# Who shares a wide tile with whom: group sums and gate batches in a fused attention and MLP kernel

## The chip, the cores and the metric

The kernel runs on one core of a Trainium2 chip. The metric is the device time of one execution in microseconds (us); a comparison uses the median of several executions. Times inside the kernel come from one profiled execution, counted from the start of its span. TensorE appears in the profile as PE (matmuls) and PEld (weight loads), VectorE as DVE, ScalarE as ACT, GpSimd as POOL, SyncE's queue as SPq. SyncE issues nearly all transfers.

## The reference

Linear attention without a softmax, an RMS norm over each head, and then a two-layer network whose gate is `h * erf(softplus(h))`:

```python
# q, k, v: (8, 8, 576, 64); w_in: (512, 2048), w_out: (2048, 512); float64 weights for the network
kv  = np.einsum('bhsd,bhse->bhde', k, v)
out = np.einsum('bhsd,bhde->bhse', q, kv)
rms = np.sqrt(np.mean(out * out, axis=-1, keepdims=True) + 1e-06)
x   = (out / rms * g_norm)           # -> (4608, 512): rows are tokens
h   = x @ w_in
sp  = np.maximum(h, 0.0) + np.log1p(np.exp(-np.abs(h)))
g   = h * erf(sp)
y   = g @ w_out                      # (4608, 512)
```

## The kernel before

The 4608 tokens are worked through in nine groups `T` of 512 (`NG = 9`). In each group the 2048 hidden features are 16 blocks of 128, taken in batches of four (`BATCH = 4`, so `NB = 4` batches in a group). The first two groups (`FIRST = 2`) run a plain fp32 path while the weights are converted and cut into three forms; from group 2 on, and for the last batch of group 1, a product of fp32 precision is put together from three cheaper matmuls (`n_ps` takes eight matmuls, `m_ps` four).

From there on the kernel is a loop over batches `m`, with `T, b = divmod(m, 4)`. It starts at `m = 8`. In iteration `m` the hidden products of batch `m` are computed into a wide tile `h`; the gates of batch `m - 1`, made in the iteration before, are cut into forms and multiplied by their four blocks of `w_out`; and the result is added to the group's sums `es`, which are stored to the output after the group's last batch. Since the results trail by one batch, the first group that the loop stores is group 1: its sums were begun before the loop, and are finished and stored in iteration 8.

The wide tiles are of one size: 128 partitions by 4 x 512 fp32 values. There are three of them: two in the pool `wide`, given out in turns under the tag `h`, and one in the pool `acc` under the tag `e`. A tile that is given out again must wait until all that read the former contents is done.

```python
    wide = ctx.enter_context(tc.tile_pool(name="wide", bufs=2, side="right"))
    ...
            acc = ctx.enter_context(tc.tile_pool(name="acc", bufs=1))
    ...
    # the plain path: who takes a wide tile, in order of time
                    xT[T] = wide.tile([P, KC, G], FP32, name="xT", tag="h")          # T = 0, 1
                x_high = wide.tile([P, KC, G], FP32R, name="x_high", tag="h")        # group 1
                old_h = acc.tile([P, BATCH, G], FP32, name="h", tag="e")             # last batch of group 1
                    x_both = wide.tile([P, KC, G], FP32R, name="x_both", tag="h")    # group 1
                sums(*((acc, "e") if T2 < FIRST - 1 else (wide, "h")))               # groups 0 and 1

    def sums(pool, tag):
        all_e = pool.tile([P, J, DM], FP32, name="e", tag=tag)
        ...                               # es[j] = all_e[:, j], copied from o_ps[j]

    def store(T, j, e):
        if T < B:
            rows = out[T * S : T * S + G, :].rearrange("(p j) f -> p j f", j=J)
            nc.sync.dma_start(out=rows[:, j, :], in_=e)
            return
        ...

    def product(weights, moving, turns=True):     # L462 is its matmul
        ...                               # two of six PSUM banks in turns: n_ps (8 matmuls), m_ps (4)

    def result(T, b, j, g, w):
        ps = product(...)
        if b == 0:
            if j == 0:
                all_e = acc.tile([P, J, DM], FP32, name="e", tag="e")
                es.update((i, all_e[:, i]) for i in range(J))
            nc.vector.tensor_scalar(                                                 # L775
                out=es[j], in0=ps[0], scalar1=SHIFT - 1.0, scalar2=None, op0=ALU.mult
            )
        else:
            add_scaled(es[j], ps[0], SHIFT - 1.0)                                    # L440
        add(es[j], ps[1])                                                            # L445

    for m in range(first_batch, batches + 1):
        ...
        g, done = g_next, len(g_next)
        g_next = []
        if m < batches:
            h = wide.tile([P, BATCH, G], FP32, name="h", tag="h")
            s = gate_r.tile([P, BATCH, G], FP32, name="s", tag="s")
        for i in range(BATCH):
            if m < batches:
                n_ps, m_ps = hidden(T, b * BATCH + i)
            fetch(i)                                  # weight parts for later, on SyncE's queue
            if i == 0:
                for half in range(done, 2):
                    g.append(cut_upper(old_h, half))                                 # ACT, L405
            if done <= i < 2:
                cut_lower(old_h, i, g[i])                                            # DVE, L408 and L411
            if m < batches:
                nc.scalar.activation(h[:, i], n_ps, AF.Copy, scale=SHIFT - 1.0)      # L834
                add(h[:, i], m_ps)                                                   # L445
                nc.scalar.activation(s[:, i], h[:, i], AF.Softplus)                  # L836
            pieces(i + 1)                             # a piece of the next group's attention
        ...                                           # Erf of s (L840)
        for j in range(J):
            result(T2, b2, j, g, w)
            fetch(BATCH + j)
            if b2 == NB - 1:
                store(T2, j, es.pop(j))
            ...                                       # h *= s (L854), pieces of attention
        old_h = h
```

Of the kernel before, what the change touches and what calls it, by code (L numbers as in the profile page):

```python
# [39 lines left out]
FP32 = mybir.dt.float32  # L40
FP32R = mybir.dt.float32r
# [9 lines left out]
BATCH = 4  # L51
# [3 lines left out]
FIRST = 2  # L55
# [5 lines left out]
def kernel(  # L61
# [11 lines left out]
    P = 128  # L73
    B, H, S, D = q.shape
    DM, DF = moe_w_in.shape[0], moe_w_in.shape[1] // 2
    J = 4
    G = J * P
    R = S - G
    NP = H // 2
    KC = DM // P  # L80
# [6 lines left out]
    attp = ctx.enter_context(tc.tile_pool(name="attp", bufs=1))  # L87
    dram = ctx.enter_context(tc.tile_pool(name="dram", bufs=1, space=bass.MemoryType.DRAM))

    wide = ctx.enter_context(tc.tile_pool(name="wide", bufs=2, side="right"))  # L90

    room, early_room, low_room = (ctx.enter_context(ExitStack()) for _ in range(3))
    first_w = room.enter_context(tc.tile_pool(name="first_w", bufs=1, side="right"))
# [162 lines left out]
    def weights():  # L256

        w_next("split")
        w_next("join")
        w_next("load")  # L260


    xT, x_forms, tails = {}, {}, {}
# [5 lines left out]
    def attention(T, p, pools=None):  # L269
# [94 lines left out]
        def norm():  # L364
            ms, u, r = (st.pop(name) for name in ("ms", "u", "r"))
            nc.vector.scalar_tensor_tensor(
                out=u, in0=ms, scalar=EPS, in1=u, op0=ALU.add, op1=ALU.mult
            )
            nc.vector.scalar_tensor_tensor(
                out=u, in0=u, scalar=3.0, in1=r, op0=ALU.subtract, op1=ALU.mult  # L370
            )
            if T < FIRST:
                if T not in xT:
                    xT[T] = wide.tile([P, KC, G], FP32, name="xT", tag="h")
                x = xT[T][:, p, :]
            else:
                x = st["x"] = x_new.tile([P, G], FP32, name="x", tag="x")
            nc.vector.scalar_tensor_tensor(
                out=x,
                in0=st.pop("o"),  # L380
                scalar=gm_col,
                in1=u,
                op0=ALU.mult,
                op1=ALU.mult,
            )
# [153 lines left out]
# [4 lines that stand above are left out]
            e = es[j] = all_e[:, j]  # L543
            if j % 2:
                nc.scalar.copy(e, o_ps[j])
            else:
                nc.vector.tensor_copy(out=e, in_=o_ps[j])
# [87 lines left out]
    def due(k):  # L635

        i = w_at["join"] + k
        ahead = 1 if LAG - 2 <= n < LAG + BATCH else 2
        return i < len(w_order) and w_order[i][0] <= n + ahead

    def gates(n):
        nc.vector.tensor_tensor(out=hs[n], in0=hs[n], in1=ss[n], op=ALU.mult)  # L642

    for n in range(FIRST * FC + 1):
        T, f = divmod(n, FC)
        if n == FC:
            early_room.close()
            late = ctx.enter_context(tc.tile_pool(name="late", bufs=1))
            x_new = ctx.enter_context(tc.tile_pool(name="x_new", bufs=1))
            acc = ctx.enter_context(tc.tile_pool(name="acc", bufs=1))  # L650
            w_in_p = ctx.enter_context(tc.tile_pool(name="w_in_p", bufs=BATCH))
            low = low_room.enter_context(tc.tile_pool(name="low", bufs=1))
            forms = late.tile([P, 3, KC, G], FP32R, name="x_forms0")
            x_forms[FIRST] = [forms[:, i] for i in range(3)]
        if T < FIRST:
            if f == 0:
                steps = pieces_of(T + 1)
            if due(1):
                weights()
            for key in list(w_new)[:2]:  # L660
                w_lower(*key)
            for piece in steps[f][0]:
                piece()
        while due(0):
            weights()
        done = n - LAG + 1
        if T == 0 and done >= 0:
            gates(done)
        if T == FIRST - 1:
            if f == 0:  # L670
                x_high = wide.tile([P, KC, G], FP32R, name="x_high", tag="h")
                x_low = low.tile([P, KC, G], FP32R, name="x_low")
                for i in range(0, KC, 2):
                    upper(xT[T][:, i : i + 2], x_high[:, i : i + 2])
                for i in range(0, KC, 2):
                    lower_only(xT[T][:, i : i + 2], x_high[:, i : i + 2], x_low[:, i : i + 2])
        if T == FIRST - 1 and f >= WHOLE:
            n_ps, m_ps = hidden(T, f, turns=False)
        elif T < FIRST:

            if n > 1:
                plain[n] = ps_h.tile([P, G], FP32, name="h_ps", tag="h")
                blocks = [(n, c) for c in range(KC)]
            elif n == 0:
                for i, (pool, tag) in enumerate(((ps_at, "at"), (ps_o, "o0"))):
                    plain[i] = pool.tile([P, G], FP32, name="h_ps", tag=tag)
                blocks = [(i, c) for c in range(KC - 1) for i in range(2)] + [(0, KC - 1)]
            else:
                blocks = [(1, KC - 1)]
            for i, c in blocks:  # L690
                nc.tensor.matmul(  # L691
                    plain[i],
                    lhsT=w_in_sb[:, c, i % FC * P : i % FC * P + P],
                    rhs=xT[T][:, c, :],
                    start=(c == 0),
                    stop=(c == KC - 1),
                )
        if T < FIRST:
            if n == whole:
                old_h = acc.tile([P, BATCH, G], FP32, name="h", tag="e")  # L700
            h = hs[n] = old_h[:, n - whole] if n >= whole else unit("h_sb")
            s = ss[n] = unit("s_sb")
            if n in plain:
                nc.scalar.copy(h, plain.pop(n))
            else:
                nc.scalar.activation(h, n_ps, AF.Copy, scale=SHIFT - 1.0)
                add(h, m_ps)
            if T == FIRST - 1:
                if f == 1:
                    x_both = wide.tile([P, KC, G], FP32R, name="x_both", tag="h")  # L710
                    for i in range(0, KC, 2):
                        both_only(x_high[:, i : i + 2], x_low[:, i : i + 2], x_both[:, i : i + 2])
                    x_forms[T] = x_high, x_low, x_both
                gates(done)
                for key in list(w_new):
                    w_lower(*key)
                for key in to_cut[f]:
                    w_upper(*key)
            nc.scalar.activation(s, h, AF.Softplus)
            if n == 0:  # L720
                w_next("split")
            for piece in steps[f][1]:
                piece()
            if f % BATCH == BATCH - 1:
                for i in range(n - BATCH + 1, n + 1):
                    nc.scalar.activation(ss[i], ss[i], AF.Erf)
                softplus_table()
            if T == FIRST - 1:
                load_parts("in", {FC - 3: 2, FC - 2: 1, FC - 1: 1}.get(f, 0))
        if n >= LAG:  # L730
            T2, f2 = divmod(n - LAG, FC)
            last = n - LAG in (FC - 1, whole - 1)
            project(f2, hs[n - LAG], last)
            if last:
                sums(*((acc, "e") if T2 < FIRST - 1 else (wide, "h")))
                if T2 == 0:
                    for j in range(J):
                        store(T2, j, es.pop(j))
        if T < FIRST:
            for piece in steps[f][2]:  # L740
                piece()
# [23 lines left out]
    def result(T, b, j, g, w):  # L765

        ps = product(
            lambda form, f: g[j // 2][:, form, f, j % 2 * P : j % 2 * P + P],
            lambda form, f: w[f][:, form],
        )  # L770
        if b == 0:
            if j == 0:
                all_e = acc.tile([P, J, DM], FP32, name="e", tag="e")
                es.update((i, all_e[:, i]) for i in range(J))
            nc.vector.tensor_scalar(  # L775
                out=es[j], in0=ps[0], scalar1=SHIFT - 1.0, scalar2=None, op0=ALU.mult
# [4 lines that stand above are left out]
# [5 lines left out]
    for m in range(first_batch, batches + 1):  # L786
        T, b = divmod(m, NB)
        todo = []
        if T + 1 < NG:
            todo = list(attention(T + 1, b))  # L790
            if b == 0:
                side = late_r if T % 2 == FIRST % 2 else late
# [3 lines left out]
        def piece():  # L796
            if todo:
                todo.pop(0)()
# [20 lines left out]
        g, done = g_next, len(g_next)  # L819
        g_next = []  # L820
        if m < batches:
            h = wide.tile([P, BATCH, G], FP32, name="h", tag="h")
            s = gate_r.tile([P, BATCH, G], FP32, name="s", tag="s")
        for i in range(BATCH):
            if m < batches:
# [17 lines left out]
        T2, b2 = divmod(m - 1, NB)  # L843
# [50 lines left out]
```

## Time and profile before

| | before |
|---|---|
| device time, median of 3 | 954.99 us (953.88 to 955.01) |
| span of the profiled execution | 952.2 us, 11746 instructions |
| TensorE matmuls busy | 929.1 us, 98% |
| VectorE busy | 740.4 us, 78% |
| ScalarE busy | 616.1 us, 65% |
| bytes moved by DMA | 259.78 MB, mean 273 GB/s |

How to read it: a busy share near 100% says which engine is in use all along, and not that every microsecond of it is needed. Where a stage of the kernel is paced by TensorE, time can only be won by removing matmul work or idle stretches of TensorE. The chain of waits follows the work that ended last back from the end, at each step to what released it. The list of waits names who stood idle for whom. A table of windows gives the busy time of each engine in chosen stretches of time, with TensorE's granted clock and the share of the 16 DMA engines in use.

### The profile page before, as it was taken

Reading aid. Unit: us, or ns where it says so; the run is one execution under the profiler, and the core shown is the slowest. Engines: PE = TensorE matmul, PEld = TensorE weight load, DVE = VectorE, ACT = ScalarE, POOL = GpSimd, SP = SyncE. Lnnn points to the kernel's source line nnn. Section 1 sums busy time; section 2 is a strip of 40 time slices with the busy share of each in tenths; the row PEclk is TensorE's granted clock in tenths of the full one; section 3 lists DMA queues with packets and bytes.
Section 4 is the critical chain, followed back from the end, with each engine's and each line's share of the span. In section 5 each row is a group of like instructions: output and inputs, shape, how many; then the busy total and the mean of one; then the engine's idle time right before and its main releaser. Section 6 shows DMA issues by size and latency. Waiting matters only on the chain.

```text
span 952.2 us, 11746 instructions
## 1 busy us (share of the span) xinstructions
PE 929.1 (98%) x4272; PEld 684.7 (72%) x4272; DVE 740.4 (78%) x1054; ACT 616.1 (65%) x825; POOL 2.4 (0%) x10
## 2 busy tenths in 40 slices
PE   6999999999998999999999999999999999999998
PEld 4444445665686788888888888888888788878886
DVE  3979958888575888888888888887887877777667
ACT  3889876777665666666666666666666666665552
POOL 1000000000000000000000000000000000000000
PEclk9999999999999999999999999999999999999999
DMA  9856505899699888898899988988896779768872
GB/s 256 276 163 212 167 9 218 307 347 337 212 356 339 275 286 282 289 315 301 290 304 309 303 293 314 322 290 283 290 337 251 264 256 348 283 248 304 338 272 65
DMA packets 111842, 259.78 MB, mean 273 GB/s; under 512 B 43864, under 2 KB 69544, under 8 KB 111784
## 3 DMA queue, kind: packets, MB, share of 16 engines
q1 hardware_dynamic: 110152, 256.73, 78.1%
q10 hardware_dynamic: 1568, 2.29, 0.8%
q8 instruction: 34, 0.56, 0.2%
q14 instruction: 24, 0.20, 0.1%
q0 software_dynamic: 64, 0.00, 0.0%
HBM read 224.40 MB, written 34.60 MB: 272 GB/s over the span
## 4 chain that ended last, share of the span: by engine, by line
PE 83%; ACT 6%; DVE 6%; DMA 3%; SPq 1%; issue 1%; DVEq 0%; ACTq 0%
PE n_ps L462 42%; PE m_ps L462 21%; PE o_ps L520 8%; PE h_ps L691 3%; PE se_ps L325 3%; PE kv_ps L297 2%; PE qt_ps L319 2%; DMA out_dram<-e 1%; DMA w_in_parts<-w_in 1%; SPq L136 1%; ACT w_e L215 1%; ACT L103 1%; DVE h L445 1%; ACT w_m L219 1%; DMA q_sb<-in_q_dram 1%
## 5 line engine op out<-in xcount | busy, mean ns | idle before, releaser
L462 PE MATMUL n_ps<-x_forms,w_in_parts 128*128 128x512 f32 x896 | 234.9, 404 | 5.0 <-ACT h L834 3.4
L462 PE MATMUL n_ps<-w_out_parts,g_forms 128*128 128x512 f32 x928 | 231.3, 391 | 0.0
L462 PEld LDWEIGHTS n_ps<-x_forms,w_in_parts 128*128 128x128 f32 x896 | 167.6, 189 | 49.4 <-issue 9.3
L462 PEld LDWEIGHTS n_ps<-w_out_parts,g_forms 128*128 128x128 f32 x928 | 174.2, 188 | 38.4 <-issue 1.7
L836 ACT ACTIVATE s<-h 128x512 f32<-128x512 f32 x112 | 71.1, 635 | 180.5 <-DVE h L445 180.5
L445 DVE TENSOR_TENSOR h<-m_ps,h 128x512 f32<-128x512 f32 x116 | 79.8, 688 | 68.3 <-ACT h L834 48.9
L462 PE MATMUL m_ps<-w_out_parts,g_forms 128*128 128x512 f32 x464 | 124.2, 389 | 0.0
L462 PE MATMUL m_ps<-x_forms,w_in_parts 128*128 128x512 f32 x448 | 120.0, 390 | 0.0
L520 PE MATMUL o_ps<-w_out_sb,h_sb 128*128 128x512 f32 x224 | 100.8, 593 | 0.3 <-DVE h_sb L642 0.3
L462 PEld LDWEIGHTS m_ps<-w_out_parts,g_forms 128*128 128x128 f32 x464 | 87.1, 188 | 18.1
L462 PEld LDWEIGHTS m_ps<-x_forms,w_in_parts 128*128 128x128 f32 x448 | 84.3, 188 | 17.8
L445 DVE TENSOR_TENSOR e<-m_ps,e 128x512 f32<-128x512 f32 x116 | 80.2, 692 | 17.9 <-PE m_ps L462 10.5
L440 DVE SCALAR_TENSOR_TENSOR e<-n_ps,e 128x512 f32<-128x512 f32 x88 | 60.3, 685 | 37.6 <-PE n_ps L462 37.5
L520 PEld LDWEIGHTS o_ps<-w_out_sb,h_sb 128*128 128x128 f32 x224 | 42.3, 190 | 48.9 <-issue 46.6
L834 ACT ACTIVATE h<-n_ps 128x512 f32<-128x512 f32 x112 | 65.6, 586 | 13.4 <-DMA out_dram<-e 9.5
L411 DVE SCALAR_TENSOR_TENSOR g_forms<-g_forms 128x1024 fp32r<-128x1024 f32 x58 | 71.1, 1225 | 2.0
L408 DVE TENSOR_TENSOR g_forms<-h,g_forms 128x1024 fp32r<-128x1024 f32 x58 | 70.6, 1217 | 1.8 <-ACT g_forms L405 1.4
L405 ACT ACTIVATE g_forms<-h 128x1024 fp32r<-128x1024 f32 x58 | 58.9, 1060 | 12.4 <-PE m_ps L462 9.8
L854 DVE TENSOR_TENSOR h<-h,s 128x1024 f32<-128x1024 f32 x56 | 65.9, 1218 | 0.7 <-ACT s L840 0.7
L691 PE MATMUL h_ps<-xT,w_in_sb 128*128 128x512 f32 x144 | 64.9, 594 | 0.8 <-DVE w_in_sb L240 0.6
L106 ACT ACT_TABLE_LOAD x44 | 56.5, 1283 | 0.7
L840 ACT ACTIVATE s<-s 128x1024 f32<-128x1024 f32 x56 | 56.2, 1052 | 0.3
(98 smaller groups left out, 1014.9 us busy)
## 6 DMA issues: line engine op xcount, KB each, us to landing
w_out_parts<-w_out SPq DMA_DIRECT2D x116, 768.0 KB
w_in_parts<-w_in SPq DMA_DIRECT2D x112, 768.0 KB
w_in<-w_new SPq DMA_DIRECT2D x16, 768.0 KB
q_sb<-in_q_dram SPq DMA_DIRECT2D x32, 256.0 KB
w_raw<-in_moe_w_out_dram SPq DMA_DIRECT2D x8, 1024.0 KB
out_dram<-e SPq DMA_DIRECT2D x32, 256.0 KB
k_sb<-in_k_dram SPq DMA_DIRECT2D x28, 287.5 KB
v_sb<-in_v_dram SPq DMA_DIRECT2D x28, 287.5 KB
```

The costliest lines, as they stand in the source:

```text
L106: nc.scalar.preload_act_table_set("softplus")
L405: nc.scalar.activation(high, x, AF.Copy, scale=1.0 + 2.0**-13)
L408: nc.vector.tensor_tensor(out=low, in0=x, in1=high.bitcast(FP32), op=ALU.subtract)
L411: nc.vector.scalar_tensor_tensor(out=both, in0=low.bitcast(FP32), scalar=SHIFT, in1=high.bitcast(FP32), op0=ALU.mult, op1=ALU.add,)
L440: nc.vector.scalar_tensor_tensor(out=out_, in0=ps, scalar=scale, in1=out_, op0=ALU.mult, op1=ALU.add)
L445: nc.vector.tensor_tensor(out=out_, in0=ps, in1=out_, op=ALU.add)
L462: nc.tensor.matmul(ps, lhsT=weights(form, k), rhs=moving(form, k), start=(form == forms[0] and k == 0), stop=(form == forms[-1] and k == 3),)
L520: nc.tensor.matmul(o_ps[j], lhsT=g[:, j * P : j * P + P], rhs=w_out_sb[:, f, :], start=(f == 0), stop=last,)
L691: nc.tensor.matmul(plain[i], lhsT=w_in_sb[:, c, i % FC * P : i % FC * P + P], rhs=xT[T][:, c, :], start=(c == 0), stop=(c == KC - 1),)
L834: nc.scalar.activation(h[:, i], n_ps, AF.Copy, scale=SHIFT - 1.0)
L836: nc.scalar.activation(s[:, i], h[:, i], AF.Softplus)
L854: nc.vector.tensor_tensor(out=part(h, half), in0=part(h, half), in1=part(s, half), op=ALU.mult)
```

## The change

The two tiles of the pool `wide` get names of their own, `a` and `b`, in place of turns under one tag. In the plain path each user gets the tile that the turns had given it. In the loop the users are dealt out anew. The group sums always take tile `a`. The gate batches `h` take tile `b` when `m` is even and the tile of `acc` when `m` is odd. What this is for: a batch `h` shall not be given a tile out of which sums are still being stored.

```diff
-    wide = ctx.enter_context(tc.tile_pool(name="wide", bufs=2, side="right"))
+    wide = ctx.enter_context(tc.tile_pool(name="wide", bufs=1, side="right"))
@@ the plain path
-                    xT[T] = wide.tile([P, KC, G], FP32, name="xT", tag="h")
+                    xT[T] = wide.tile([P, KC, G], FP32, name="xT", tag="ab"[T])
-                x_high = wide.tile([P, KC, G], FP32R, name="x_high", tag="h")
+                x_high = wide.tile([P, KC, G], FP32R, name="x_high", tag="a")
-                    x_both = wide.tile([P, KC, G], FP32R, name="x_both", tag="h")
+                    x_both = wide.tile([P, KC, G], FP32R, name="x_both", tag="b")
-                sums(*((acc, "e") if T2 < FIRST - 1 else (wide, "h")))
+                sums(*((acc, "e") if T2 < FIRST - 1 else (wide, "a")))
@@ def result
-                all_e = acc.tile([P, J, DM], FP32, name="e", tag="e")
+                all_e = wide.tile([P, J, DM], FP32, name="e", tag="a")
@@ the loop over batches
-            h = wide.tile([P, BATCH, G], FP32, name="h", tag="h")
+
+            pool, tag = (acc, "e") if m % 2 else (wide, "b")
+            h = pool.tile([P, BATCH, G], FP32, name="h", tag=tag)
```

No operation, transfer or order of instructions is changed; what changes is the address of some operands and, with it, who waits for whom.

## The prediction

> **What bounds the kernel now.** I read the page first, then the list of waits, the chain of waits around the one wait that the change aims at, windows cut at the batches of the loop, and the timelines of TensorE and VectorE there. The page says that the whole is paced by TensorE:
>
> ```profile
> span 952.2 us, 11746 instructions
> PE 929.1 (98%) x4272; PEld 684.7 (72%) x4272; DVE 740.4 (78%) x1054; ACT 616.1 (65%) x825; POOL 2.4 (0%) x10
> ```
>
> The list of waits has many entries for DVE and ACT, which cost nothing while PE runs on. Three lines belong together, each of one single occurrence: ACT stood 9.5 us before L834 for a store of sums, and PE then stood 3.4 us for that L834 (its weight load 3.8 us).
>
> ```profile
> ACT h L834 <- DMA out_dram<-e: 9.5, 1, 9.5
> ...
> PEld n_ps L462 <- ACT h L834: 3.8, 1, 3.8
> ...
> PE n_ps L462 <- ACT h L834: 3.4, 1, 3.4
> ```
>
> The chain (start us, us, what) shows the same place as the only piece longer than 3 us after 280 us that is not PE's: the last store, issued at 283.21, lands 9.85 us later, and L834 follows at once.
>
> ```profile
> 283.21 9.85 DMA out_dram<-e
> 293.21 0.61 ACT h L834
> ```
>
> Next, windows cut where PE begins the hidden products of iterations 8, 9, 10, 11 and 12 (256.18, 280.90, 311.80, 336.53, 361.36). The reader is to see that iteration 9 alone takes 30.90 us, and that PE's clock is below 1 in it:
>
> ```profile
> 256.18:280.90 24.72, 24.72 (x129) 19.98 (x128) 18.66 (x28) 16.81 (x23) 0.00 (x0) 1.00 0.85 297
> 280.90:311.80 30.90, 27.00 (x131) 21.18 (x129) 19.11 (x27) 15.83 (x21) 0.00 (x0) 0.94 0.93 344
> 311.80:336.53 24.73, 24.73 (x130) 19.98 (x128) 20.17 (x30) 16.08 (x22) 0.00 (x0) 1.00 0.85 281
> 336.53:361.36 24.83, 24.83 (x131) 20.09 (x129) 20.19 (x29) 15.94 (x22) 0.00 (x0) 1.00 0.86 295
> ```
>
> Slices of 5 us place the loss of clock and the state of the DMA engines (last two columns: share, GB/s):
>
> ```profile
> 285.00:290.00 5.00, 5.00 (x23) 3.83 (x22) 1.46 (x2) 0.00 (x0) 0.00 (x0) 1.00 1.04 422
> 290.00:295.00 5.00, 1.59 (x6) 0.98 (x5) 1.16 (x2) 1.03 (x2) 0.00 (x0) 0.90 0.97 374
> 295.00:300.00 5.00, 5.00 (x18) 3.98 (x18) 3.42 (x6) 2.37 (x6) 0.00 (x0) 0.76 0.61 182
> ```
>
> PE's timeline shows the stop, and the eight matmuls after it in 3.68 us where iteration 8 has 1.98; VectorE's shows the first write into the next group's sums:
>
> ```profile
> 265.57 1.98 PE L462 MATMUL n_ps<-x_forms,w_in_parts 128*128 128x512 f32 x8
> ...
> 293.86 3.68 PE L462 MATMUL n_ps<-x_forms,w_in_parts 128*128 128x512 f32 x8 [3.41 <-ACT h L834]
> ```
>
> ```profile
> 301.68 0.68 DVE L775 TENSOR_SCALAR e<-n_ps 128x512 f32<-128x512 f32 x1
> ```
>
> [...] PE stands 3.41 us, and the clock averages 0.90 and 0.76 in the two slices above. So the stop costs its own length and a slow stretch after it. [...] a 256 KB store that takes 9.85 us: SyncE issued two 768 KB weight parts at 281.31, just ahead of it, and the engines were at 1.04 of their time and 422 GB/s.
>
> **The change, part by part.**
> 1. The plain path: the turns under one tag gave xT of group 0 the first tile, xT of group 1 the second, then x_high the first, x_both the second, the sums of group 1 the first. The names a, b, a, b, a give the same. Cost 0. Iteration 8's batch took the second, now b: 0 again.
> 2. Iteration 9's batch took the first tile in the old order, and that held the sums of group 1, whose four stores were issued at 274.01, 276.12, 280.92 and 283.21. Now it takes the tile of acc, whose last content, the last batch of group 1, was read by the cuts of iteration 8. They ended at 264.2 on DVE. So L834 no longer waits. ACT is free at 283.69 (L405 at 281.67, two in 2.02 us) and n_ps is complete at 282.9, so L834 can start 9.5 us sooner. VectorE's L445 stands behind the first cut on DVE, which ends at 286.5, as in every iteration (in iteration 10 it starts 6.6 us after PE's start; 280.90 + 6.6 = 287.5). PE needs its bank for the fourth hidden product at 290.46, so it does not stop.
> 3. What that is worth on PE: 30.90 us less the length of an iteration with the same work. Iteration 11 is the fitting one, since both have 131 matmul records and end with the transposition of q_last (L305), and it takes 24.83. Saved: 30.90 - 24.83 = 6.07 us. By parts: 3.41 us of standing still; the clock, (1 - 0.90) x 5 + (1 - 0.76) x 5 = 1.7 us (the timeline's pair gives 3.68 - 1.98 = 1.7 too); and 0.45 us in front of the transposes of q at 311.39, which waited for L378 because ACT and DVE ran late. These are 5.56 us. The remaining 0.5 us are small gaps and the modelled ends of matmuls, which I don't place; I take the difference of the iterations.
> 4. Sums of groups 2 to 8 move from the tile of acc to a, batches from two tiles in turns to b and acc. Each keeps the count it had: one tile for sums, two for batches, with the same readers. Cost 0 in the 27 remaining iterations.
> 5. New in iteration 9: the first L775 of group 2 writes into a, the tile being stored. This is the wait of part 2 in a later place, and the first rival below.
>
> After 312 us PE stands for others 1.4 us in all by the list of waits, so nothing downstream absorbs a shift. Everything after iteration 9 moves forward by 6.07: 952.2 - 6.1 = 946.1 us of span, and 954.99 - 6.07 = 948.9 us of device time.
>
> **The rivals.** First, L775 takes over the wait. In iteration 8 the first read of a result stands 14.13 us after PE's start (270.31 - 256.18), so L775 would be ready at 280.90 + 14.1 = 295.0, and the store was down by 293.2: 1.8 us to spare. In front of that store lie only transfers issued before the stop could make any difference, so its landing should hold. If it were late, DVE has 1.6 us of idle time behind the next result (iteration 8, 1.61 before the second L440), and L378 ends at 279.5, 1.0 us before PE's transposes at 280.49 need it. It would thus have to land later than about 297.5 to be felt. For it speaks only that the DMA engines are full there. It would give 949 to 951.
>
> Second, the transfers become the bound. From 275 to 295 they run at 1.02 or more in most slices, and the stop gave them time to catch up; the share falls to 0.61 after 295. Without the stop, the last two weight parts for iteration 9's results (issued from 281.31, ahead of the store and so down by about 293) are needed from 280.90 + 12.1 = 293.0, the third and fourth about 0.9 and 1.4 us into it. Counting the packets of weight parts in order of issue, I find the last of them through near 290.5. For iteration 10, two parts of w_in are issued at 297.61 and 298.55, behind slow issues of k and v that owe nothing to the stop, with two parts of w_out and k, v among them: 4 x 0.79 + 0.58 = 3.7 MB, at 0.42 MB per us some 9 us, so down by about 307.5. They are needed at 305.73 + 6.25 = 312.0 and 314.7. In both places there is room, in the first only 1 to 3 us. If it fails, PE stops again for 1 to 4 us, perhaps with the half clock: 950 to 954.
>
> Third, the new addresses or the new dealing of tiles make a wait in each iteration, say a batch in acc that waits for its reader two iterations back. The reader is then a whole iteration (24.7 us) past. I see nothing for it; 27 waits of 0.5 us would give 962.
>
> **Range and chances.** The sum gives 948.9. The three times before lie within 1.1 us of each other. I give the first two rivals together 15%, each with a loss of 1 to 3 us, and the third 2%. So the range is 947.8 to 950.8. A gain over 2% would need 19 us, three times all that iteration 9 loses: 1%. A loss over 2% is as unlikely: 1%.
>
> **What would show it.** Right: no wait of L834 for out_dram; iteration 9 at 24.8 us; a granted clock of 1.00 throughout from 285 to 300; the wait of PE for L834 gone; the first L775 of group 2 near 295.0; the same 24.7 and 24.8 in iterations 10 and 11. Wrong in the first rival's way: DVE waiting for out_dram in front of L775 and PE standing near 304. In the second's: PE waiting for w_out_parts near 294 or w_in_parts near 312. The prediction fails outright if iterations after the tenth come out longer than before.

## The result, and the profile after

The changed kernel takes 947.95 us (median of 4; 947.50 to 948.04), the kernel before 954.49 us in the same comparison (median of 4; 953.88 to 955.01). The ratio is 0.9931, with a 95% interval of 0.9914 to 0.9948: a gain of 0.7%, clear of noise and under 2%.

The page of the changed kernel, its totals and the line of the copy that had waited (it is L836 now, two lines lower):

```profile
span 945.7 us, 11743 instructions
PE 926.8 (98%) x4272; PEld 683.3 (72%) x4272; DVE 740.5 (78%) x1054; ACT 615.7 (65%) x825; POOL 2.4 (0%) x10
...
L836 ACT ACTIVATE h<-n_ps 128x512 f32<-128x512 f32 x112 | 65.5, 585 | 3.9 <-PE n_ps L462 3.8
```

In the kernel before, the page has for the same copy:

```profile
L834 ACT ACTIVATE h<-n_ps 128x512 f32<-128x512 f32 x112 | 65.6, 586 | 13.4 <-DMA out_dram<-e 9.5
```

The idle time in front of it fell from 13.4 to 3.9 us, and out_dram is no longer what ended most of it. Windows cut where PE begins iterations 8, 9, 10 and 11 of the changed kernel (us, busy time of PE, PEld, DVE, ACT and POOL, granted clock, DMA share, GB/s):

```profile
255.65:280.41 24.76, 24.76 (x130) 19.98 (x128) 18.67 (x28) 16.81 (x23) 0.00 (x0) 1.00 0.88 319
280.41:305.24 24.83, 24.83 (x131) 20.09 (x129) 20.06 (x29) 15.90 (x21) 0.00 (x0) 1.00 0.95 349
305.24:329.97 24.73, 24.73 (x130) 19.98 (x128) 19.94 (x30) 15.90 (x21) 0.00 (x0) 1.00 0.94 323
```

Iteration 9 takes 24.83 us, the length of iteration 11 in the kernel before. PE is busy all through it, and the clock is 1.00. The fourth hidden product and the first result follow without a stop, and the first write into the new group's sums waits for PE alone (timelines of PE and of DVE, changed kernel):

```profile
289.80 1.98 PE L462 MATMUL n_ps<-x_forms,w_in_parts 128*128 128x512 f32 x8
291.61 1.07 PE L462 MATMUL m_ps<-x_forms,w_in_parts 128*128 128x512 f32 x4
292.52 1.98 PE L462 MATMUL n_ps<-w_out_parts,g_forms 128*128 128x512 f32 x8
```

```profile
294.53 0.69 DVE L775 TENSOR_SCALAR e<-n_ps 128x512 f32<-128x512 f32 x1 [0.57 <-PE n_ps L462]
```

Where the time went: of the 6.5 us between the two spans, 6.07 lie in iteration 9 (30.90 less 24.83). From iteration 10 to the end the profiled executions take 952.2 - 311.80 = 640.4 and 945.7 - 305.24 = 640.5 us. The other half microsecond lies ahead of iteration 8, which begins at 256.18 and 255.65, where neither code nor dealing differs. In the profiled executions of this study that start lies between 255.58 and 257.99, so I take it for the spread of the plain path.

### The profile page after: what moved, and what is told of

Read it like the earlier page. It is cut to its first block, busy times and chain, and to the rows that moved or that the text cites. A ratio compares the mean times of both kernels' runs of the same rounds, so it can differ in the third digit from the quotient of the medians.

```text
span 945.7 us, 11743 instructions
## 1 busy us (share of the span) xinstructions
PE 926.8 (98%) x4272; PEld 683.3 (72%) x4272; DVE 740.5 (78%) x1054; ACT 615.7 (65%) x825; POOL 2.4 (0%) x10
## 4 chain that ended last, share of the span: by engine, by line
PE 88%; ACT 5%; DVE 5%; DMA 1%; issue 1%; DVEq 0%
PE n_ps L462 45%; PE m_ps L462 23%; PE o_ps L520 8%; PE h_ps L691 3%; PE se_ps L325 3%; PE kv_ps L297 2%; PE qt_ps L319 2%; ACT w_e L215 1%; ACT w_m L219 1%; DMA q_sb<-in_q_dram 1%; PE ms_ps L347 1%; PE ms_ps L346 1%; PE ms_ps L351 1%; ACT L103 1%; ACT s_sb L719 1%
## 5 line engine op out<-in xcount | busy, mean ns | idle before, releaser
L836 ACT ACTIVATE h<-n_ps 128x512 f32<-128x512 f32 x112 | 65.5, 585 | 3.9 <-PE n_ps L462 3.8
```

## The experiments

The theory: all of the gain is the one wait of iteration 9's batch for the stores out of its tile. The rivals: the new places and dealing of tiles bring a part of it, and the wait that moved to the group's sums takes some back. All ratios are to the kernel before on the same chip. It had a median of 954.66 us in runs 1, 2, 3 and 6 and 954.26 in runs 4, 5, 7 and 8. A ratio can differ from the quotient of the medians by up to 0.0007.

**1 and 2. One edit in both kernels.** The four stores of group 1 in iteration 8 read the tile of acc in place of the sums. The same number of bytes is stored, but group 1's output rows hold other values. In the kernel before, this frees the tile of iteration 9's batch; in the changed kernel, it ties that tile up.

```diff
             if b2 == NB - 1:
-                store(T2, j, es.pop(j))
+                e = es.pop(j)
+                store(T2, j, old_h[:, j] if m == first_batch else e)
```

> The kernel before, dealing of tiles untouched; only the four stores of group 1 in iteration 8 read the tile of acc (the last gate batch of group 1) in place of the sums, so group 1's output rows hold other values; bytes and transfers are the same. Theory (all of the gain is the one wait of iteration 9's batch for the stores out of its tile): the wait is gone although every tile has its old place, iteration 9 takes 24.8 us, clock 1.00, and the time is 947.5 to 949. Rival (the new places or the new dealing in the 27 later iterations bring a part): 951 to 954.5. Rival (first write of group 2's sums takes the wait over): over 949.5, with DVE waiting for out_dram, since that write goes to the tile of acc here.

Measured: 947.69 us (947.09 to 948.39), ratio 0.9929 (0.9912 to 0.9945). Iteration 9 of the old dealing (window cut at its ends) and its first write of sums (DVE timeline):

```profile
281.00:305.83 24.83, 24.83 (x131) 20.09 (x129) 20.05 (x29) 15.91 (x21) 0.00 (x0) 1.00 0.93 334
```

```profile
295.12 0.69 DVE L775 TENSOR_SCALAR e<-n_ps 128x512 f32<-128x512 f32 x1 [0.58 <-PE n_ps L462]
```

The old dealing with the wait taken away is as fast as the new one. The 24.83 us of iteration 9 are the same number as in the changed kernel, and the write of sums waits for PE alone although its tile is the one being stored here.

> The changed kernel with the same edit: the four stores of group 1 read the tile of acc, which is the one that iteration 9's batch is given now; group 1's output rows hold other values. Theory: the loss comes back, L836 waits for out_dram, PE stands about 3 us and then runs at half clock, 952 to 954.5 (a little under the kernel before, because the stores need not wait for VectorE's additions here and can be issued 1 to 3 us sooner). Rival (new places, new dealing): stays at 947.5 to 949.

Measured: 954.46 us (952.39 to 955.07), ratio 0.9997 (0.9981 to 1.0013). The loss is back, by the list of waits at the same instruction (here the stored tile is called h):

```profile
ACT h L836 <- DMA out_dram<-h: 8.5, 1, 8.5
...
PE n_ps L462 <- ACT h L836: 2.3, 1, 2.3
```

Iteration 9 takes 29.81 us in the profiled execution, with a clock of 1.00 in it: the stop is 2.3 us where I expected about 3, and the half clock that I expected is not there. That execution took 952.39 us; the other three, with a clock of 0.996 to 0.998 over their spans, took 954.44 to 955.07. So the edit turns each kernel into the other. The new places and the 27 later iterations are worth nothing that shows.

**3. The last store ahead of the weights.** In the kernel before, the store of j = 3 is issued before the two weight parts that had stood in front of it.

```diff
-            fetch(BATCH + j)
+            ahead = m == first_batch and j == J - 1
+            if not ahead:
+                fetch(BATCH + j)
             if b2 == NB - 1:
                 store(T2, j, es.pop(j))
+            if ahead:
+                fetch(BATCH + j)
```

> The kernel before, with the last store of group 1 issued ahead of the two weight parts that stood before it in SyncE's queue. Nothing is left out. Theory (the store's 9.85 us are mostly queueing behind 1.5 MB of weights, 3.7 us at 0.42 MB per us, plus 0.9 us of issue): it lands near 288.5, PE stands under 1 us or not at all, 948 to 950. Rival (the landing is slow of itself, because all 16 engines are full, whatever the order of issue): lands near 292, PE stands 2 to 3 us, 952 to 954.

Measured: 950.10 us (949.32 to 952.53), ratio 0.9959 (0.9942 to 0.9977). The ACT timeline, then PE's with what is left of the stop:

```profile
289.33 0.60 ACT L834 ACTIVATE h<-n_ps 128x512 f32<-128x512 f32 x1 [6.17 <-DMA out_dram<-e]
```

```profile
289.98 2.11 PE L462 MATMUL n_ps<-x_forms,w_in_parts 128*128 128x512 f32 x8
...
296.40 0.51 PE L346 MATMUL ms_ps<-sq_hi,mean_w 128*128 128x512 f32 x1 [0.68 <-DVE sq_hi L338]
297.12 0.50 PE L347 MATMUL ms_ps<-sq_lo,mean_w 128*128 128x512 f32 x1 [0.22 <-DVE sq_lo L339]
...
305.98 0.80 PE L297 MATMUL kv_ps<-v_sb,k_sb 116*64 116x64 f32 x20 [0.17 <-DVE u L366]
...
307.49 0.66 PE L319 MATMUL qt_ps<-ident,q_sb 128*128 128x128 f32 x4 [0.45 <-DVE x L378]
```

Counted from PE's start of iteration 9, L834 starts 8.95 us in (289.33 - 280.38), in the kernel before 12.31 (293.21 - 280.90): 3.36 us sooner. Of this, 0.9 us is an earlier issue of the store (281.8, 1.4 us in, against 2.31) and about 2.5 a shorter time from issue to the copy (7.5 against 10.0), where I had put 3.7 on the two weight parts. So the order of issue does count, but most of the store's time under way is not these two parts. The long stop is gone. But iteration 9 still takes 27.52 us (PE starts at 280.38 and 307.90), 2.7 more than undisturbed. VectorE runs late, and PE waits for it four times, for 1.52 us by the brackets. Each of these waits costs a little more than its bracket: the first matmul after a pause shows 0.50 or 0.51 us where the undisturbed timeline has 0.39. My 948 to 950 left this lag out, and the measured median is 0.1 us above it.

**4 to 6. How much room the moved wait has.** In the changed kernel, the last store of group 1 is held back to three places in iteration 9: behind the load of q, of k, or of v. The edit of the latest, in short:

```diff
-                store(T2, j, es.pop(j))
+                if m == first_batch and j in (3,):
+                    held.append((T2, j, es.pop(j)))
+                else:
+                    store(T2, j, es.pop(j))
@@ iteration 9, after the attention piece with the loads
             pieces(i + 1)
+            while i == 2 and held:
+                store(*held.pop(0))
```

> The changed kernel, last store of group 1 held back until iteration 9's load of q is issued (near 287.5), ahead of k and v. Nothing is left out. Behind two more weight parts and q it should land about 1 to 2.5 us after L775 could start. Account of the slack (L775 may start up to about 17 us after PE's start of iteration 9 before PE feels it; without a wait it starts 14.1 us after): DVE waits 0.5 to 2.5 us for out_dram, PE loses nothing, 947.5 to 948.5. Rival (each microsecond of wait in front of L775 goes through to PE): 948.5 to 950.5.

> The changed kernel, last store of group 1 held back until iteration 9's loads of q and k are issued (near 292). Nothing is left out. It should land 17 to 20 us after PE's start of iteration 9. Account of the slack: DVE waits 3 to 6 us, PE loses that less 3 us: 0 to 3 us and no half clock, 948 to 951. Rival (each microsecond goes through): 951 to 954.

> The changed kernel, with the last store of group 1 held back until iteration 9's k and v loads are issued, near 294.9. Nothing is left out. It doubles the moved wait: first write of group 2's sums (L775) must wait for a store that lands near 297 to 299. My account gives VectorE's idle time and the slack in front of PE's transposes as room until about 297.5: 948 to 949.5, DVE waits 2.5 to 4.5 us for out_dram, PE at most 1.5 us. Rival (each microsecond of wait in front of L775 goes through to PE): 950.5 to 952.5.

Measured, with the start of L775 counted from PE's start of iteration 9 and its loss from 24.83 us:

| store held behind | issued | wait of DVE | L775 starts | iteration 9 | loss there | device time | ratio (95%) |
|---|---|---|---|---|---|---|---|
| nothing (the change) | 281.83 | none | 14.12 us in | 24.83 | 0 | 947.95 | 0.9931 (0.9914 to 0.9948) |
| q | 288.16 | 3.7 us | 17.19 | 24.92 | 0.09 | 947.82 | 0.9939 (0.9923 to 0.9955) |
| k | 295.40 | 5.5 us | 19.00 | 26.73 | 1.90 | 950.74 | 0.9967 (0.9947 to 0.9986) |
| v | 296.31 | 8.6 us | 22.13 | 30.21 | 5.38 | 954.47 | 1.0001 (0.9986 to 1.0016) |

VectorE's timeline, then PE's, in the last of them:

```profile
303.19 0.69 DVE L775 TENSOR_SCALAR e<-n_ps 128x512 f32<-128x512 f32 x1 [8.57 <-DMA out_dram<-e]
```

```profile
303.93 2.14 PE L462 MATMUL n_ps<-w_out_parts,g_forms 128*128 128x512 f32 x8 [1.95 <-DVE e L775]
...
308.99 0.80 PE L297 MATMUL kv_ps<-v_sb,k_sb 116*64 116x64 f32 x20 [2.00 <-DVE u L366]
...
310.50 1.11 PE L319 MATMUL qt_ps<-ident,q_sb 128*128 128x128 f32 x4 [0.45 <-DVE x L378]
```

By the run behind q the room ends near 17.1 us after PE's start (17.19 less the 0.09 lost): up to there 3.7 us of waiting on DVE cost 0.1 us. Beyond it each microsecond costs about one (19.00 - 17.1 = 1.9, as lost behind k; 22.13 - 17.1 = 5.0 against 5.38 behind v). Behind v, the next iteration loses another 1.2 us (25.96 at a clock of 0.95), so the whole gain is gone. The account of the room held and its rival fell, above all behind q. What I had misjudged was the transfer. Behind q, DVE waited 3.7 us in place of 0.5 to 2.5, and the issue alone kept SyncE's queue busy for 5.08 us:

```profile
288.16 5.08 SPq L535 DMA_DIRECT2D out_dram<-e  x1
```

Behind v, the time lies outside both ranges that I had given: the store was issued 1.4 us later than I took it to be, and was 6.75 us under way by the chain of waits, where I had allowed 2 to 4.

**7. A longer stop in the kernel before.** The last store goes behind one of iteration 9's loads of weight parts.

```diff
-            fetch(i)
+            if not (m == first_batch + 1 and i == 1):
+                fetch(i)
+            if held:
+                fetch(1)
+                store(*held.pop(0))
```

> The kernel before, with one of iteration 9's loads of weight parts drawn ahead of the last store of group 1. Nothing is left out. The store is issued about 1.3 us later and behind another 768 KB (1.9 us at 0.42 MB per us), so it lands 2 to 3 us later. Theory (loss is the stop plus one slow window of fixed cost): PE stands 5.5 to 6.5 us, 1.7 us more for the clock, in all 956.5 to 958. Rival (what counts is not this wait): 954.5 as before.

Measured: 954.89 us (953.59 to 956.30), ratio 1.0012 (0.9993 to 1.0031): not told apart from the kernel before, and short of what I expected. Timelines of ACT and of PE:

```profile
294.02 0.60 ACT L838 ACTIVATE h<-n_ps 128x512 f32<-128x512 f32 x1 [10.31 <-DMA q_sb<-in_q_dram]
```

```profile
294.67 3.78 PE L462 MATMUL n_ps<-x_forms,w_in_parts 128*128 128x512 f32 x8 [4.18 <-ACT h L838]
298.25 1.91 PE L462 MATMUL m_ps<-x_forms,w_in_parts 128*128 128x512 f32 x4
299.96 2.38 PE L462 MATMUL n_ps<-w_out_parts,g_forms 128*128 128x512 f32 x8
```

(The bracket names a load of q. The instruction reads no q, and the store is what it has to wait for; the releaser is an inference from semaphores.) Counted from PE's start of iteration 9 (280.94), the copy starts 0.8 us later than in the kernel before, where I reckoned 2 to 3, and PE stands 4.18 us in place of 3.41. The time is that of the rival, 954.5; but with the stop only 0.8 us longer, the run does not decide between the two. The store is issued 1.1 us later (284.38, 3.44 us in) and needs 9.64 us from issue to the copy, against 10.0. So the 768 KB issued ahead of it cost nothing that shows in this one execution, while in run 3 the 1.5 MB were worth about 2.5 us. Why the two differ stays open. The slow matmuls last longer than after the stop of 3.41: the next m_ps group takes 1.91 us where 1.07 is usual, and the half clock lasts twice as long as in the kernel before (last section), where I had reckoned with one slow stretch of fixed cost. Iteration 9 takes 32.15 us.

**8. Both together.** The edit of run 3, in the changed kernel.

> The changed kernel with the last store of group 1 ahead of the two weight parts, the edit that shortened the wait of the kernel before. Nothing is left out. Theory: the store waits on nobody's path any more, so an earlier landing is worth nothing: 947.5 to 948.5. Rival (the moved wait or the weight parts still cost something): a shift of over 1 us either way.

Measured: 947.40 us (947.27 to 947.92), ratio 0.9934 (0.9915 to 0.9953); iteration 9 takes 24.83 us. Once nobody waits for the store, an earlier landing is worth nothing that shows: the change itself had 0.9931.

## Why the prediction was right

- The place and the bound. It said that one wait in iteration 9 carries all of it and that the rest of the loop only shifts. Iteration 9 went from 30.90 to 24.83, to the hundredth what iteration 11 had foretold, and the stretch behind it kept its length within 0.1 us. Runs 1 and 2 show that the wait is the cause, not the places.
- The size. Foretold was 948.9, measured 947.95. In the traces the term of 6.07 us is right. Of the 0.95 us that are over, 0.50 is the base: the kernel before had 954.99 in the three executions known then and 954.49 in the comparison. The rest, 6.54 measured against 6.07, is well inside the interval of the ratio (about 1.6 us either way). That the sum came so close to the median is thus in part luck.
- The clock term, 1.7 us, was read from one execution and held for that one: its trace has half the clock for 3.41 us (last section), and half of that is 1.7. In the 14 runs of the kernel before that were taken beside the experiments, three have a clock of 0.999 or 1.000 and take 951.93 to 952.64 us; the other eleven have 0.996 to 0.998 and take 954.02 to 955.87. Their medians, 952.55 and 954.66, differ by 2.1 us. So the slow stretch costs about 2 us by my estimate from these two medians, and it does not come in every execution. A fixed 1.7 was too simple, though near the mean.
- The 0.5 us that I had not placed. In run 2's profiled execution the brackets of PE in iteration 9 add up to 2.33 + 0.68 + 0.22 + 0.17 + 0.45 = 3.85 us, and the iteration loses 29.81 - 24.83 = 4.98 at full clock. Some 1.1 us are thus lost around five stops beyond their brackets, as in run 3. The kernel before has two of these stops, for the copy and in front of the transposes. In run 2 the two lose 0.30 us (the m_ps group behind the first starts 2.63 us later than in the changed kernel, counted from PE's start, with a bracket of 2.33) and 0.23 us. That the same restarts make up the 0.5 of the kernel before fits, but is argued from this, not shown.
- First rival, the wait that moves to L775. Foretold was L775 ready at 295.0 with the store down by 293.2, and room until about 297.5, which is 16.6 us after PE's start. Measured: it starts 14.12 us in, waits for PE alone, and the room ends near 17.1. So the moved wait is real, runs 4 to 6 make it bind, and in the change it has 3 us of room behind it.
- Second rival, the transfers. From 285 to 290 the engines are as full as before (1.02 of their time and 420 GB/s), and PE waits for no weight part in the iterations after (from 300 us on it waits 1.4 us in all, for x_forms of DVE and ACT). The weights arrived in time. One figure of the working is off: iteration 10's fourth product starts 9.4 us in, so at 315.1 and not at 314.7, which leaves more room. How near the weights come to being late is not shown.
- Third rival, a wait in each iteration. Iterations 10 and 11 keep their lengths (24.73 and 24.83 us), and run 1 equals the change.

## What to carry to other kernels

When buffers are given out in turns, look at the first turn after a change of phase: a user with a short life (a batch) can be handed the buffer that a slow reader (here a store that was 9.85 us under way) still holds, once, and nothing in the averages shows it. Cut the trace at the loop's iterations and compare lengths; the one that is too long carries the size of the gain, and here an iteration with the same work gave it to the hundredth. Then ask where the wait goes when the buffer is given to another, and measure the room that it has there by delaying it step by step.

## What the runs showed of the hardware

The clock of TensorE after a stop varies from run to run. In the kernel before, the trace records half the clock for 3.41 us, from 294.00 on. Windows of that length ahead of the half clock and in it, for the kernel before, then for runs 7 and 6 (the second number is PE's busy time, the third from the end the clock):

```profile
290.59:294.00 3.41, 0.14 (x1) 0.14 (x2) 0.16 (x1) 0.60 (x1) 0.00 (x0) 1.00 1.02 406
294.00:297.42 3.42, 3.42 (x9) 2.65 (x10) 3.39 (x4) 1.12 (x2) 0.00 (x0) 0.50 0.48 151
```

```profile
290.48:293.89 3.41, 0.01 (x1) 0.00 (x0) 0.00 (x0) 0.00 (x0) 0.00 (x0) 1.00 1.01 375
293.89:297.31 3.42, 2.64 (x6) 2.15 (x7) 2.62 (x3) 1.71 (x3) 0.00 (x0) 0.50 0.48 132
297.31:300.72 3.41, 3.41 (x9) 2.64 (x8) 1.87 (x5) 1.60 (x3) 0.00 (x0) 0.50 0.95 279
```

```profile
307.04:310.45 3.41, 1.06 (x21) 0.80 (x21) 3.34 (x6) 0.00 (x0) 0.00 (x0) 1.00 0.98 411
310.45:313.86 3.41, 3.36 (x10) 2.87 (x11) 3.17 (x5) 2.84 (x4) 0.00 (x0) 0.50 0.43 139
```

In run 2, where PE stood 2.33 us up to 292.18, slices of 5 us show no loss of clock:

```profile
285.00:290.00 5.00, 4.86 (x21) 3.38 (x19) 0.90 (x1) 0.00 (x0) 0.00 (x0) 1.00 1.02 421
290.00:295.00 5.00, 2.82 (x12) 2.36 (x13) 2.80 (x3) 1.71 (x3) 0.00 (x0) 1.00 0.80 294
295.00:300.00 5.00, 4.10 (x17) 2.84 (x16) 3.30 (x8) 2.72 (x5) 0.00 (x0) 1.00 0.83 235
```

Half the clock came behind windows in which PE was busy for 0.14, 0.01 and 1.06 us, and it lasted for one such window in the kernel before and in run 6, for two in run 7. The length of the longest stop does not tell these runs apart from run 2: in run 6 no stop of iteration 9 was longer than 2.00 us, and the half clock came; in run 2 one was 2.33 us, and it did not. Only one execution of each kernel has a trace, so what lowers the clock in some executions of the kernel before and of run 2, and not in others, is not shown.

A store of 256 KB was long under way: 9.85 us in the kernel before, issued behind weight parts while the engines moved 422 GB/s from 285 to 290 us and 374 from 290 to 295, and 6.75 us in run 6 behind q, k and v, while they moved 223 GB/s from 295 to 300 us and 382 from 300 to 305. That the weight parts issued ahead of it hold a store up was my estimate; run 3 puts about 2.5 us of the 10.0 from issue to copy on them, run 7 shows no cost of the kind, and what the rest is made of is not shown.
